# A causal attention and MLP-mixer kernel: loads of the opening in another sequence, and early work ordered to fit

## The chip, the cores and the metric

The kernel runs on one core of a Trainium2 chip. The metric is the device time of one execution in microseconds (us). The core has five engines that work side by side, each through its own queue in order: TensorE (PE, matrix products, with PEld for its weight loads), VectorE (DVE), ScalarE (ACT), GpSimd (POOL) and SyncE (SP), and DMA engines that move data between device memory and on-chip memory. PE writes its products into PSUM banks, which DVE and ACT empty.

## The reference

There are 8 batches of 576 positions with 8 heads of 64. Attention is causal by blocks of 64; its result goes through a token mixer and a channel mixer.

```
block_i, block_j = pos[:, None] // 64, pos[None, :] // 64
scores = q @ k^T / sqrt(64);  scores = where(block_i >= block_j, scores, -1e9)
attn   = exp(scores - max);   attn = attn / (sum(attn) + 1e-9)
x      = (attn @ v), heads side by side                 # 8 x 576 x 512
h      = relu(x^T @ w_tok1) @ w_tok2                     # 576 -> 256 -> 576
u      = x + h^T
out    = u + relu(u @ w_ch1) @ w_ch2                     # 512 -> 1536 -> 512
```

All inputs and the output are float32. Products are in bf16.

## The kernel before

The work is held as about 1590 numbered operations (`P.add`), each with its engine or a choice of engines, the operations it depends on, the PSUM banks it takes and gives back, and a function that issues its instructions. A table, `ORDER`, written out as a string, says in which order they are issued, on which engine (S, P, D, A, T for SP, POOL, DVE, ACT, PE), and in which banks: letters a to d are the four banks `mm`, e to h the four `late`, s and t two double banks in which the first scores are made. The late banks are the same memory as the double ones, and can be used only when the exps of the last double bank are done. `Plan.placed` walks through the table. Since each engine works in order, an operation that waits holds back all that stands behind it on its engine.

Batches go through the same steps, with the steps of neighbouring batches mixed. The loads of q, k (L418) and V (L468) stand on POOL's queue, which also converts them to bf16; so do the loads of the weights: w_tok1 and w_tok2 (L479), w_ch1 in eight pieces (L502) and w_ch2 in three (L511). Only the very first pieces of q and k go another way. The rest of the attention:

- q and k are transposed on DVE (`STREAM_TRANSPOSE`, L442). A score set (L568) holds the products of four heads (two at the start) for a part of the keys.
- exp is done on ACT (L587 for the double banks, L774 for the others) into `e_sb`. The part of `e_sb` that the mask leaves out is copied and cleared (L596, L601) on DVE or POOL.
- A head's output is the product of `e_sb` and V (L618, the odd ends in L671). DVE takes the reciprocal of the sum (L638, L693) and scales (L644, L699) into `x_sb`.

The mixer:

- `token_up`: x times w_tok1 (L809, L813), relu into `aT` on ACT (L795) or DVE (L797).
- batch 0 makes u^T on PE directly (L842, L857, emptied by L874 on DVE or its like on ACT). The others make u = x + h^T (L904, added on DVE in L919) and then transpose it (L991 for batch 1).
- channel up: u times w_ch1 (L1032 for batch 0), relu into `gT`.
- channel down: batch 0 uses a scheme of seven products for a 2 by 2 split (L1366), with sums of blocks of w_ch2 (`weight_sums`, L1318, four instructions on DVE into `wd_sb`, which need all three loads of w_ch2) and of `gT` (L1348); the later channel-up products use sums of blocks of w_ch1 (L1063) in the same way.

At the start PE runs products on zeros (`raise_clock`): one run of 11 products of 512 columns (L371), and single fillers of 256 columns (L378), 37 of which the table places between the first real products.

Of the kernel before, what the change touches and what calls it, by code (L numbers as in the profile page):

```python
# [27 lines left out]
class Plan:  # L28
# [73 lines left out]
    47Tb 48Tb 49Ta 50Ta 37P 51Ta 52Ta 53Ta 54Ta 55Ta 56Ta 35P 57Ta 7D 174Tst 175T 34P 195A 58Ta 59Ta 60Ta  # L102
    61Ta 196A 62Ta 38P 197D 63Ta 31D 64Ta 65Ta 66Ta 176A 199Tt 36P 177A 178D 67Ta 179D 68Ta 33D 69Ta 255P 70Ta 200A
    180Ts 27D 198P 71Ta 72Ta 40P 73Ta 181A 29D 182Tt 157P 74Ta 75Ta 76Ta 183A 77Ta 201Ts 43P 78Ta 79Ta 80Ta 253D
    202A 42P 214Tt 254D 188Tb 189T 41P 215A 184Tc 11D 233Ts 6D 190D 191D 258P 192Td 211Ta 234A 220Tt 216P 256D 39P
    185T 257D 221A 81Tb 218Ts 155P 212D 213D 207Tb 235D 208T 186D 219A 158P 187D 237Tt 193D 209D 156P 203Ta 210D
    204T 238A 194D 239Ts 261P 205D 206D 164P 8D 240A 236D 269Tcbda 424P 271A 163P 281Tefgh 270A 166P 259D 273A 217D
    226Tb 283A 227T 284A 222Tc 223T 228D 241Ta 242T 282A 229D 165P 249Tf 224D 245Tg 285A 225D 162P 246T 230Tb 243D
    244D 339Tc 159P 250D 231D 232D 337Ta 251D 247D 161P 340A 260D 272A 276Tbfeh 338D 348Tc 262D 160P 278A 349T 263D
    345Ta 280A 346T 248D 277A 341Td 350D 421P 301Tgbfh 274D 347D 264P 343Tc 342D 303A 275D 351Ta 304A 265P 352T 344D  # L110
    305A 425D 354Td 355T 302A 313Tcbfh 279A 356D 306P 387Tg 353A 267P 426D 384Td 315A 388T 266P 316A 404Ta 385T 317A
    268P 408Tb 314A 381Te 386D 405A 416Tf 427P 409D 390Tc 389A 307P 391T 333D 430P 372Td 392A 308Tabhg 167P 373T
    311A 334D 382T 168P 310A 369Tc 309A 370T 169P 417A 375Tb 335D 434P 312A 378Ta 379T 383A 433P 366Th 374A 367T
    422D 371A 436P 400Td 423D 376T 380A 289Tc 377A 295Ta 290D 298Tf 368A 291D 330Tb 296D 401A 297D 292Tc 299D 286Tg
    331D 332D 438Tadeh 300D 287D 293D 288D 324Tb 440A 294D 357Tf 325D 439A 321Tc 326D 363Tg 428D 442A 364T 322D 441A
# [67 lines left out]
def kernel(  # L183
# [95 lines left out]
    WARM, KEEP = 11, 110  # L279
    HALF_UP, FAST_UP = 1, 4  # L280

    def uT_of(b):
# [1284 lines left out]
```

## Time and profile before

Three runs took 283.47, 284.16 and 284.64 us (median 284.16).

| | before |
|---|---|
| profiled execution, its own time | 284.69 us |
| its span, from first to last instruction | 282.9 us |
| granted clock of PE (share of full speed) | 1.0 |
| batch 2's first score set starts on PE | 43.69 us |
| the first of the four sums of w_ch2 starts on DVE | 50.80 us |
| batch 0's channel down starts on PE | 55.75 us |
| bytes that the POOL queue moved | 17.49 MB |

In a row of the timeline the first number is the start in us, the second the time from the start of the first to the end of the last instruction that the row takes together; then the engine, the line of the kernel, the operation, its output and inputs with their shapes, and how many. A bracket at the end holds the idle time of the engine ahead of it, and what ended it. Rows of DMA issues give the size and the time from issue to landing. In the table of stretches each engine has its busy time and the number of its instructions.

### The profile page before, as it was taken

To read this page: it belongs to the slowest core of one execution; us is meant where nothing else is said; L and a number is where in the kernel's file an instruction comes from. 1 tells how busy PE (TensorE), PEld (TensorE's weight loads), DVE (VectorE), ACT (ScalarE), POOL (GpSimd) and SP (SyncE) were. 2 spreads that over 40 slices of the span, in tenths; PEclk is the share of its full clock that TensorE was granted. 3 is DMA by queue.
4 is the path that set the end of the run, shared out by engine and by line. 5 is a ranking of instruction groups with operands and counts; after the bars stand their busy time and mean duration, and the time that the engine had idled before them with its cause. 6 is when DMAs were issued, how large, how long until landed. Compare 5 with 4: busy or idle time off the path is not lost.

```text
span 282.9 us, 9352 instructions
## 1 busy us (share of the span) xinstructions
PE 275.3 (97%) x3982; PEld 204.0 (72%) x3982; DVE 238.9 (84%) x515; ACT 179.2 (63%) x331; POOL 72.7 (26%) x126
## 2 busy tenths in 40 slices
PE   7899999999999999999999999999999999999994
PEld 3466556588776788986877658756789876568884
DVE  3688669999889998999998979859896997579984
ACT  3798788953998856897879866274533744652200
POOL 8895870511631351063232221000000000000000
PEclk9999999999999999999999999999999999999999
DMA  7999999954979492999598594100044502200157
GB/s 163 160 178 192 202 190 206 152 92 86 142 87 139 87 150 56 250 109 170 66 118 139 56 188 60 70 10 19 0 84 95 196 0 76 75 1 2 74 151 224
DMA packets 64890, 31.95 MB, mean 113 GB/s; under 512 B 53200, under 2 KB 55888, under 8 KB 64848
## 3 DMA queue, kind: packets, MB, share of 16 engines
q0 software_dynamic: 44896, 17.49, 53.6%
q1 hardware_dynamic: 19520, 13.21, 18.2%
q8 instruction: 31, 0.51, 0.7%
q10 hardware_dynamic: 432, 0.66, 0.7%
q14 instruction: 11, 0.09, 0.1%
HBM read 35.85 MB, written 9.44 MB: 160 GB/s over the span
## 4 chain that ended last, share of the span: by engine, by line
PE 87%; DMA 4%; ACT 3%; POOL 3%; DVE 1%; issue 1%; POOLq 0%; DVEq 0%
PE late L1366 23%; PE mm L1105 8%; PE mm L1232 7%; PE mm L1366 7%; PE late L1232 6%; PE mm L568 6%; PE late L1105 6%; DMA qk_sb<-in_k_dram 4%; PE mm L618 4%; PE mm L809 3%; PE mm L904 2%; PE late L904 2%; PE late L618 2%; PE mm L1032 2%; ACT e_sb L774 2%; PE late L809 2%
## 5 line engine op out<-in xcount | busy, mean ns | idle before, releaser
L774 ACT ACTIVATE e_sb<-mm 128x512 bf16<-128x512 f32 x82 | 46.6, 606 | 13.1 <-PE late L568 9.4
L774 ACT ACTIVATE e_sb<-late 128x512 bf16<-128x512 f32 x86 | 48.5, 609 | 9.0 <-PE late L568 8.2
L442 DVE STREAM_TRANSPOSE qk_sb<-qk_sb 128x288 int32<-128x288 int32 (+1 forms) x65 | 41.8, 694 | 4.9 <-DMA qk_sb<-in_q_dram 1.8
L468 POOL DMA_DIRECT2D vals<-in_v_dram x45 | 36.9, 832 | 4.5 <-PE mm L618 2.4
L1366 PEld LDWEIGHTS <-gT 128*128 128x128 bf16 x336 | 32.0, 98 | 5.6 <-issue 0.4
L1366 PEld LDWEIGHTS <-sums 128*128 128x128 bf16 x324 | 31.3, 98 | 5.3 <-issue 0.4
L568 PEld LDWEIGHTS <-qk_sb 32*64 32x64 bf16 (+1 forms) x1152 | 19.0, 103 | 14.8 <-issue 11.1
L568 PE MATMUL mm<-qk_sb 32*64 32x64 bf16 (+7 forms) x504 | 26.9, 277 | 0.1
L618 PEld LDWEIGHTS <-e_sb 128*128 128x128 bf16 x640 | 23.1, 97 | 5.3 <-issue 2.2
L568 PE MATMUL late<-qk_sb 32*64 32x64 bf16 (+7 forms) x504 | 26.2, 283 | 0.6 <-issue 0.3
L1366 PE MATMUL late<-wd_sb,gT 128*128 128x256 bf16 x168 | 20.7, 273 | 0.0
L1366 PE MATMUL late<-wd_sb,sums 128*128 128x256 bf16 x168 | 20.6, 273 | 0.0
L1105 PEld LDWEIGHTS <-ws_sb 128*128 128x128 bf16 x192 | 18.2, 98 | 3.1 <-issue 0.9
L618 PE MATMUL mm<-vals,e_sb 128*128 128x65 bf16 x450 | 19.8, 193 | 0.5 <-DMA vals<-in_v_dram 0.3
L644 DVE TENSOR_TENSOR x_sb<-mm,rinv 128x256 bf16<-128x256 f32 x45 | 18.7, 422 | 1.3
L1412 DVE TENSOR_TENSOR o_sb<-late,u_sb 128x512 f32<-128x512 f32 x22 | 15.0, 684 | 3.6 <-PE late L1366 3.6
L1232 PEld LDWEIGHTS <-ws_sb 128*128 128x128 bf16 x120 | 11.7, 98 | 8.6 <-issue 0.2
L1105 PEld LDWEIGHTS <-wc_sb 128*128 128x128 bf16 x144 | 15.3, 114 | 1.5 <-issue 0.4
L1366 PE MATMUL late<-wc_sb,gT 128*128 128x256 bf16 x132 | 16.2, 273 | 0.0
L596 POOL COPY vals<-e_sb 128x256 bf16<-128x256 bf16 (+1 forms) x11 | 4.3, 393 | 39.7 <-ACT e_sb L774 39.6
L400 ACT COPY mm<-late 128x512 f32<-128x512 f32 (+1 forms) x16 | 9.1, 570 | 8.1 <-PE late L1232 5.4
L795 ACT ACTIVATE gT<-mm 128x512 bf16<-128x512 f32 x21 | 12.6, 616 | 1.9 <-PE mm L1105 0.9
(198 smaller groups left out, 630.7 us busy)
## 6 DMA issues: line engine op xcount, KB each, us to landing
out_dram<-o_sb SPq DMA_DIRECT2D x19, 256.0 KB, 3.0
qk_sb<-in_k_dram POOLq DMA_DIRECT2D x14, 288.0 KB, 6.0
qk_sb<-in_q_dram POOLq DMA_DIRECT2D x14, 288.0 KB, 5.9
vals<-in_v_dram POOLq DMA_DIRECT2D x28, 128.0 KB, 4.5
out_dram<-o_sb SPq DMA_DIRECT2D x7, 512.0 KB, 3.8
wc_sb<-in_moe_w_ch_dram POOLq DMA_DIRECT2D x8, 192.0 KB, 7.5
wc_sb<-in_moe_w_ch_dram POOLq DMA_DIRECT2D x3, 512.0 KB, 10.5
vals<-in_v_dram POOLq DMA_DIRECT2D x15, 64.0 KB, 5.3
```

The source lines that it names most:

```text
L442: nc.vector.transpose(dst[:, 0:S, :] .rearrange("p s e -> p (s e)") .bitcast(I32) .rearrange("p (a k) -> p k a", k=NB)[:, k0:k1], raw2.bit ...
L468: nc.gpsimd.dma_start(out=t[128 - p : 128, J, hs, 0:64], in_=src)
L568: nc.tensor.matmul(out=home(n)[rows, c : c + w], lhsT=bar[r, 0] if j is None else kT[i][r, keys, par], rhs=bar[r, 1] if j is None else qT[ ...
L618: nc.tensor.matmul(out=u[:, I, 0:65], lhsT=e[:, h, c : c + 128], rhs=vt[:, J, head, 0:65], start=(J == 0), stop=(J == I),)
L644: nc.vector.tensor_tensor(out=xt[:, 0:4, 64 * head : 64 * head + 64], in0=u[:, :, 0:64], in1=ri[:, 0:4].to_broadcast([128, 4, 64]), op=MULT,)
L774: nc.scalar.activation(dst, bank_of(x), EXP, scale=scale)
L795: nc.scalar.activation(dst, src, RELU)
L809: nc.tensor.matmul(out=ps, lhsT=w1_sb[:, c, tt : tt + 255 : 2], rhs=xt[:, c, cols], start=(c == 0), stop=False)
L1105: nc.tensor.matmul(out=bank_of(bank)[:, 256 * o_ : 256 * o_ + 256], lhsT=x(o_, m), rhs=y[:, :, m, :], start=opens, stop=m == 1, skip_group ...
L1232: nc.tensor.matmul(out=bank_of(bank)[:, 128 * c : 128 * (c + step)], lhsT=x(m), rhs=y[:, c : c + step, m, :], start=opens, stop=m == 1, sk ...
L1366: nc.tensor.matmul(out=bank_of(bank)[:, 256 * i : 256 * i + 256], lhsT=x[:, kk, 128 * i : 128 * i + 128], rhs=y[:, kk], start=first and i ...
L1412: nc.vector.tensor_tensor(out=dst, in0=src, in1=other, op=ADD)
```

## The change

The first 392 of the 1518 places of the table are written in another order; behind them the operations follow as before, with other bank letters. No operation is added or taken away, and the sequence on SP is the same. In addition the first 22 of the single fillers issue two products of 128 columns instead of one of 256. The code after the table is three lines shorter, and two behind the fillers: L1318 before is L1316 after, L618 is L616.

The diff, with the table cut to its first rows:

```
 ORDER = """
     13S 22P 24P 5P 9D 2D 3P 16S 44Ta 12P 19S 10P 4P 30P 14D 15D 17A 32P 1D 26P 18D 20A 28P 0A 45Tb 23D 25D 21D 252P 46Tb
...
@@ -276,7 +273,7 @@
     EARLY = ("mm", "full")
     BANK = ("mm", "late mm", "full", "late")
     SEED = ("full", "late", "mm", "late mm")
-    WARM, KEEP = 11, 110
+    WARM, KEEP, HALVED = 11, 110, 22
     HALF_UP, FAST_UP = 1, 4
 
     def uT_of(b):
@@ -374,11 +371,12 @@
         for n in range(KEEP):
             bank = {"covers": False}
 
-            def emit(o, bank=bank):
-                nc.tensor.matmul(
-                    out=bank_of(bank)[:, 0:256], lhsT=zeros[:, 0:128], rhs=zeros[:, 0:256],
-                    start=True, stop=True,
-                )
+            def emit(o, bank=bank, w=128 if n < HALVED else 256):
+                for c in range(0, 256, w):
+                    nc.tensor.matmul(
+                        out=bank_of(bank)[:, c : c + w], lhsT=zeros[:, 0:128], rhs=zeros[:, c : c + w],
+                        start=c == 0, stop=True, skip_group_check=c > 0,
+                    )
 
             P.add(
                 "PE", 0.11, emit, pads["zeros"], 1e6, take=[(BANK, bank)], give=[bank], at=5.0 + 0.12 * n, until=20.0,
```

On POOL's queue, the loads from batch 0's V on (`vals`), with the token weights (`w1_sb`, `w1o_sb`, `w2_sb`) and batch 1's second pair of k and q. Before:

```order
L479 DMA w2_sb_72<-in_moe_w_tok2_dram 128x1152
L468 DMA vals_62<-in_v_dram 64x4x64
L468 DMA vals_62<-in_v_dram 128x4x64 x2
L418 DMA qk_sb_61<-in_k_dram 128x1152
L596 COPY vals_62<-e_sb1 128x128
L468 DMA vals_62<-in_v_dram 128x4x64
L479 DMA w1_sb_70<-in_moe_w_tok1_dram 128x4x256
L479 DMA w1o_sb_71<-in_moe_w_tok1_dram 64x256
L479 DMA w1_sb_70<-in_moe_w_tok1_dram 64x256
L418 DMA qk_sb_61<-in_q_dram 128x1152
```

After:

```order
L466 DMA vals_62<-in_v_dram 64x4x64
L466 DMA vals_62<-in_v_dram 128x4x64 x3
L477 DMA w1_sb_70<-in_moe_w_tok1_dram 128x4x256
L477 DMA w1o_sb_71<-in_moe_w_tok1_dram 64x256
L477 DMA w1_sb_70<-in_moe_w_tok1_dram 64x256
L594 COPY vals_62<-e_sb1 128x128
L477 DMA w2_sb_72<-in_moe_w_tok2_dram 128x1152
L416 DMA qk_sb_61<-in_k_dram 128x1152
L416 DMA qk_sb_61<-in_q_dram 128x1152
```

The four V loads stand together ahead of all token weights, and w_tok2, which stood ahead of them, and the load of k stand behind.

Further down on POOL's queue, w_ch1 (`wc1_sb`), batch 1's V, batch 2's k and q, and w_ch2 (`wc2_sb`). Before:

```order
L502 DMA wc1_sb_73<-in_moe_w_ch1_dram 128x768
L418 DMA qk_sb_61<-in_q_dram 128x1152
L502 DMA wc1_sb_73<-in_moe_w_ch1_dram 128x768 x7
L418 DMA qk_sb_61<-in_k_dram 128x1152
L468 DMA vals_62<-in_v_dram 128x8x64 x2
L596 COPY vals_62<-e_sb1 128x256
L468 DMA vals_62<-in_v_dram 128x8x64 x2
L468 DMA vals_62<-in_v_dram 64x8x64
L418 DMA qk_sb_61<-in_k_dram 128x1152
L601 MEMSET e_sb1 64x4x64
L418 DMA qk_sb_61<-in_q_dram 128x1152
L511 DMA wc2_sb_74<-in_moe_w_ch2_dram 128x2048 x3
```

After:

```order
L599 MEMSET e_sb1 64x2x64
L500 DMA wc1_sb_73<-in_moe_w_ch1_dram 128x768 x8
L466 DMA vals_62<-in_v_dram 128x8x64 x4
L466 DMA vals_62<-in_v_dram 64x8x64
L416 DMA qk_sb_61<-in_q_dram 128x1152
L416 DMA qk_sb_61<-in_k_dram 128x1152 x2
L416 DMA qk_sb_61<-in_q_dram 128x1152
L509 DMA wc2_sb_74<-in_moe_w_ch2_dram 128x2048 x3
```

w_ch1 is unbroken, batch 1's V follows it, and all four loads of batch 2's q and k stand behind that. The three loads of w_ch2 come after the same loads as before. The clear (`MEMSET`) of row one of the second piece was on DVE, and the clear and the copy that stood among the V loads went to DVE.

On DVE, where batch 0's heads end and the next k is transposed. Before:

```order
L644 TENSOR_TENSOR x_sb<-mm,rinv 128x4x64
L344 MEMSET vals 64x8
L601 MEMSET e_sb 64x2x32
L442 STREAM_TRANSPOSE qk_sb<-qk_sb 128x9x32
L601 MEMSET e_sb 64x2x32
L638 RECIPROCAL rinv<-mm 128x4
L644 TENSOR_TENSOR x_sb<-mm,rinv 128x4x64
```

After:

```order
L599 MEMSET e_sb 64x2x32
L341 MEMSET vals 64x8
L697 TENSOR_TENSOR x_sb<-mm,rinv 128x64
L636 RECIPROCAL rinv<-mm 128x4 x2
L642 TENSOR_TENSOR x_sb<-mm,rinv 128x4x64
L795 TENSOR_SCALAR aT<-mm 128x2x128
L636 RECIPROCAL rinv<-mm 128x4
L691 RECIPROCAL rinv<-mm 128x1
L697 TENSOR_TENSOR x_sb<-mm,rinv 128x64
L642 TENSOR_TENSOR x_sb<-mm,rinv 128x4x64 x2
L636 RECIPROCAL rinv<-mm 128x4
L440 STREAM_TRANSPOSE qk_sb<-qk_sb 128x9x32
```

The clear of `e_sb` that stood behind the transpose stands ahead of it, and the relu of the first token product (`aT`) stands between the head outputs.

On DVE, at the sums of w_ch2 (`wd_sb`) and of batch 0's `gT`, with batch 1's u behind them. Before:

```order
L797 TENSOR_SCALAR gT<-late 128x512
L1348 TENSOR_TENSOR sums<-gT 128x1536
L1318 TENSOR_TENSOR wd_sb<-wc_sb 128x1536 x2
L1318 TENSOR_TENSOR wd_sb<-wc_sb,wd_sb 128x1536 x2
L919 TENSOR_TENSOR u_sb<-mm,x_sb 128x512
L919 TENSOR_TENSOR u_sb<-late,x_sb 128x512
```

After:

```order
L795 TENSOR_SCALAR gT<-late 128x512
L1346 TENSOR_TENSOR sums<-gT 128x1536
L1316 TENSOR_TENSOR wd_sb<-wc_sb 128x1536
L795 TENSOR_SCALAR aT<-late 128x512
L1316 TENSOR_TENSOR wd_sb<-wc_sb 128x1536
L1316 TENSOR_TENSOR wd_sb<-wc_sb,wd_sb 128x1536 x2
L917 TENSOR_TENSOR u_sb<-mm,x_sb 128x512
L917 TENSOR_TENSOR u_sb<-late,x_sb 128x512
```

The relu of batch 1's second token product (`aT`), which was on ACT, stands between the first two sums of w_ch2.

On PE the scores of batch 1 stood ahead of batch 0's last heads; now heads 5 and 4 of batch 0 and the first token product stand ahead of them, and batch 1's first score set goes into the late banks.

More of the change, by code (lines that the diff above doesn't have):

```diff
@@ L106 @@
[L106 to L110, printed above, removed]
@@ L278 @@
     SEED = ("full", "late", "mm", "late mm")
-    WARM, KEEP = 11, 110
+    WARM, KEEP, HALVED = 11, 110, 22
     HALF_UP, FAST_UP = 1, 4
```

157 lines of the change are left out of this document (80 added, 77 removed).

## The prediction

> **What bounds the kernel now.** I read the page first, then a table of engine busy time by stretches of the span, then the rows of single engines at the places where TensorE (PE) stood.
>
> ```profile
> span 282.9 us, 9352 instructions
> PE 275.3 (97%) x3982; PEld 204.0 (72%) x3982; DVE 238.9 (84%) x515; ACT 179.2 (63%) x331; POOL 72.7 (26%) x126
> DMA  7999999954979492999598594100044502200157
> ```
>
> ```profile
> 20.00:33.00 13.00, 11.90 (x276) 8.24 (x273) 9.98 (x30) 10.41 (x21) 8.07 (x14) 1.00 1.18 196
> 33.00:45.00 12.00, 12.00 (x217) 7.87 (x216) 7.94 (x20) 9.93 (x20) 7.30 (x12) 1.00 1.52 195
> 45.00:57.00 12.00, 11.92 (x173) 6.47 (x171) 11.57 (x22) 11.99 (x25) 4.25 (x9) 1.00 1.44 172
> 57.00:120.00 63.00, 63.00 (x1127) 50.56 (x1125) 58.56 (x134) 46.77 (x92) 18.06 (x30) 1.00 0.91 120
> 120.00:200.00 80.00, 80.00 (x1299) 58.07 (x1296) 71.19 (x165) 56.56 (x109) 17.34 (x28) 1.00 0.66 90
> ```
>
> The first two numbers of a stretch are its length and PE's busy time. From 57 to 200 us PE has no idle at all, and its clock column is 1.00 everywhere. So the end of the kernel is: the time at which PE enters that dense stretch, plus a fixed amount of PE work. The change does not alter the work behind the start, so it can only move the entry. What is left to win is small: 13.00 − 11.90 = 1.10 us of idle between 20 and 33 us, nothing from 33 to 45, and 0.08 between 45 and 57. The row of DMA shares (40 slices of 7.07 us) shows nines from the second to the eighth slice: the loads run back to back from 7 to 56 us. The order of loads therefore decides only who waits, not when all of them are in.
>
> These are PE's rows where the 1.10 us lie, with two dense rows behind them for comparison (start, duration, then what ran; in brackets the idle time before it and what ended it):
>
> ```profile
> 20.18 0.55 PE L568 MATMUL mm<-qk_sb 32*64 32x320 bf16 x4
> 21.37 0.63 PE L568 MATMUL late<-qk_sb 32*128 32x512 bf16 x8 [0.30 <-ACT e_sb L587]
> 22.28 0.45 PE L618 MATMUL mm<-vals,e_sb 128*128 128x65 bf16 x9 [0.28 <-DMA vals<-in_v_dram]
> 22.93 0.81 PE L618 MATMUL mm<-vals,e_sb 128*128 128x65 bf16 x21 [0.21 <-DVE e_sb L601]
> 25.87 0.38 PE L568 MATMUL mm<-qk_sb 32*64 32x448 bf16 x1
> 26.45 0.40 PE L842 MATMUL mm<-ident,x_sb 128*128 128x128 bf16 x4
> ```
>
> Three named waits, 0.30 + 0.28 + 0.21 = 0.79 us, belong to the end of batch 0's attention: a PSUM bank that an exp frees, the last load of V, and a small clear of the probability tile. A score set that runs dense takes 26.45 − 25.87 = 0.58 us; the one at 20.18 took 21.37 − 20.18 = 1.19, which is 0.61 too long, 0.30 of it counted as idle already. So the rows show 1.10 + 0.31 = 1.4 us that PE lost there.
>
> **The change, part by part.** *V and the token weights come earlier.* The last piece of batch 0's V stood behind w_tok2 and a k load, both of 288 KB. Its issue, that of the w_tok1 loads behind it, and two later 288 KB loads in a row, which give the queue's pace (POOL's rows, then the issue-to-landing rows of the same five loads):
>
> ```profile
> 16.75 0.75 POOL L468 DMA_DIRECT2D vals<-in_v_dram  x1
> 17.48 0.75 POOL L479 DMA_DIRECT2D w_sb<-in_moe_w_tok_dram  x1
> 18.78 0.54 POOL L479 DMA_DIRECT2D w_sb<-in_moe_w_tok_dram  x1
> 34.66 0.58 POOL L418 DMA_DIRECT2D qk_sb<-in_k_dram  x1
> 35.54 0.55 POOL L418 DMA_DIRECT2D qk_sb<-in_q_dram  x1
> ...
> vals<-in_v_dram POOLq DMA_DIRECT2D x1, 64.0 KB, 5.5
> w_sb<-in_moe_w_tok_dram POOLq DMA_DIRECT2D x1, 256.0 KB, 6.1
> w_sb<-in_moe_w_tok_dram POOLq DMA_DIRECT2D x1, 32.0 KB, 5.1
> qk_sb<-in_k_dram POOLq DMA_DIRECT2D x1, 288.0 KB, 6.7
> qk_sb<-in_q_dram POOLq DMA_DIRECT2D x1, 288.0 KB, 7.4
> ```
>
> The pair landed at 34.66 + 6.7 = 41.4 and 35.54 + 7.4 = 42.9, so 288 KB take about 1.6 us. V's last piece landed at 16.75 + 5.5 = 22.3, which is the wait at 22.28; without two such loads ahead of it it lands at about 19.1. The last w_tok1 piece goes from 18.78 + 5.1 = 23.9 to about 20.7. PE now takes the heads of batch 0 and the first token product at 20.2 to 21.5, where before it took batch 1's scores. The V wait (0.28) goes. The clear's wait (0.21) goes as well: its clear stood on DVE behind a transpose of the next k and now stands ahead of it. The new wait is for w_tok1 at 20.7, when the three head operations ahead of it are just done: 0 to 0.3 us.
>
> *Batch 1's scores come later.* They now go into the late banks. Those open when ACT has finished the last paired exp:
>
> ```profile
> 17.35 3.97 ACT L587 ACTIVATE e_sb<-sc 128x1024 bf16<-128x1024 f32 x4
> ```
>
> That is 17.35 + 3.97 = 21.32, so the scores start at about 21.4, PE reaches them at about 21.5, and ACT idles for some 0.5 us instead of having scores ready. ACT is not what PE waits for in the next 10 us, except at the bank handovers. Together I take 1.1 of the 1.4 us as won by 33 us. The bounds are 0, if the new waits eat it, and 1.4.
>
> *Batch 2's q and k go back.* The four loads now stand behind w_ch1 and batch 1's V, the last one landing where the last of them did, 42.9. The first pair thus lands by 42.9 − 2 × 1.6 = 39.7. It is needed by the scores at 43.69, which with 1.1 us of lead want to start at 42.6:
>
> ```profile
> 43.69 0.33 PE L568 MATMUL mm<-qk_sb 32*64 32x320 bf16 x2
> 42.32 0.42 DVE L644 TENSOR_TENSOR x_sb<-mm,rinv 128x256 bf16<-128x256 f32 x1
> 38.25 1.25 DVE L442 STREAM_TRANSPOSE qk_sb<-qk_sb 128x288 int32<-128x288 int32 x2
> ```
>
> Two transposes took 1.25 us, so the k pair is turned at about 41.0 if DVE is free; but a scaled output of a head (0.42) stands behind them on DVE and frees a bank for these scores, with other heads between. My walk along DVE's new order ends at 42.4 to 42.9. The lead here is 0.8 to 1.1.
>
> *Where the lead meets a load that does not move.* This decides the sum. The three w_ch2 loads have the same loads ahead of them as before, so the third lands when it did. Its issue and delay, then DVE's chain that it feeds, the relu on ACT that the change moves to DVE, and two of PE's consumers:
>
> ```profile
> 38.16 0.53 POOL L511 DMA_DIRECT2D wc_sb<-in_moe_w_ch_dram  x1 [0.36 <-DMA vals<-in_v_dram]
> wc_sb<-in_moe_w_ch_dram POOLq DMA_DIRECT2D x1, 512.0 KB, 12.2
> 49.92 0.96 DVE L1348 TENSOR_TENSOR sums<-gT 128x1536 bf16<-128x1536 bf16 x1
> 50.80 1.82 DVE L1318 TENSOR_TENSOR wd_sb<-wc_sb 128x1536 bf16<-128x1536 bf16 x2
> 52.53 1.95 DVE L1318 TENSOR_TENSOR wd_sb<-wc_sb,wd_sb 128x1536 bf16<-128x1536 bf16 x2
> 54.66 0.69 DVE L919 TENSOR_TENSOR u_sb<-mm,x_sb 128x512 bf16<-128x512 f32 x1 [0.18 <-PE mm L904]
> 58.34 0.68 DVE L919 TENSOR_TENSOR u_sb<-mm,x_sb 128x512 bf16<-128x512 f32 x1
> 52.00 0.64 ACT L795 ACTIVATE aT<-mm 128x512 bf16<-128x512 f32 x1
> 55.75 0.49 PE L1366 MATMUL late<-wc_sb,gT 128*128 128x256 bf16 x3
> 59.36 0.39 PE L991 MATMUL mm<-ident,u_sb 128*128 128x128 bf16 x4
> ```
>
> The load landed at 38.16 + 12.2 = 50.4. The first weight sum (L1318) started at 50.80, when DVE came free: the load was hidden by 0.4 us. With a lead of about 1 us DVE comes free at 49.8 and waits for the load. The sum starts at about 50.4, and only 0.4 us of the lead is left on DVE. Behind that sum now stands the relu of batch 1's second token product, about 0.6 us on DVE for one of 512 columns by the pitch of its neighbours; before, ACT did it at 52.00. It ends at about 50.4 + 0.87 + 0.7 = 52.0, against 52.00 + 0.64 = 52.64 before: what needs it (a PSUM bank of a score set, a token product) may start 0.6 earlier, so this is not yet the limit. The other sums follow, then the three u rows. The 0.18 us for which DVE waited at 54.66 vanishes, and the fourth u row, which ended at 58.34 + 0.68 = 59.02, ends at 59.02 − 0.40 + 0.60 − 0.18 = 59.04, with a clear of 0.1 that also moved to DVE at 59.1. PE used it at 59.36. So PE can be at most about 0.25 us ahead there. Behind it PE is dense, and DVE in turn waits for PE: this lead stays to the end. I take 0.25 us. The bounds are −0.2, if the load lands 0.4 later, and 1.1, if DVE's chain does not hold PE.
>
> *The fillers.* Twenty-two PE fillers of 256 columns become pairs of 128. Nine of them stand ahead of a score set:
>
> ```profile
> 8.96 1.16 PE L378 MATMUL mm<-wd_sb 128*128 128x256 bf16 x9
> 10.20 0.39 PE L568 MATMUL sc<-qk_sb 32*64 32x448 bf16 x2
> 24.64 0.40 PE L809 MATMUL mm<-x_sb,w_sb 128*128 128x128 bf16 x4
> 24.88 0.19 PE L813 MATMUL mm<-x_sb,w_sb 128*128 128x64 bf16 x1
> ```
>
> Four products of 128 columns with their own weights take 24.88 − 24.64 = 0.24 us, 0.06 each, so eighteen take 1.08 us. The nine old ones took 10.20 − 8.96 = 1.24 us at most. Cost: 0. [...]
>
> **Sum.** The profiled execution took 284.69 us, 1.8 more than its span; it lies 0.53 above the median of 284.16. Its 284.69 − 0.25 = 284.44, by the median 283.9.
>
> **Rivals.** *The lead passes.* If the third w_ch2 load lands by 49.7, or PE has more slack to DVE's chain than I read, the 1.1 us stays: 283.1, and 282.8 at the bound of 1.4. For it: the loads that now stand together are larger, and the stretch with the weights (20 to 33) moved 196 GB/s against 172 from 45 to 57. Against: the bytes ahead are the same.
>
> *Slower: batch 2's first scores wait.* Their q and k landed long before use; now k lands at about 39.7 with two transposes and DVE's head outputs behind it. The point is a landing of 40.8 us: from there the scores start after 43.69, and each further us costs PE one, since the channel products that could cover have already run. At 42.0 it costs 1.2: 285.4. For it: DVE works in order, and everything behind the transpose stands too. Against: the last of the four loads landed at 42.9 already, and two of them stand behind this one.
>
> *The change wins nothing early.* If w_tok1 lands at 21.8 instead of 20.7, the first token product holds PE and, since its relu stands ahead of head outputs on DVE's queue, those too. The lead is then gone by 33 us, and the relu on DVE costs 0.2: 284.4.
>
> **How the numbers follow.** Forecast 0.46 (283.9, own range 283.5 to 284.3), the lead passes 0.25 (282.6 to 283.4), slower 0.16 (284.9 to 286), nothing early 0.13 (284.2 to 284.8). A measurement of this kernel can hardly tell less than 0.5% (1.42 us) from no change, so faster means under 282.74 and slower over 285.58. Faster: most of the lead's bound is needed, 0.16 of the 0.25 and a little for what I have not seen, 0.19. Slower: 0.10 of the 0.16 and 0.04 for what I have not seen, 0.14. The rest, 0.67, is within. The range 282.6 to 285.1 leaves out about 1 in 10 on either side.
>
> **What the profile after would show.** Right: PE's rows at 20 to 23 us without the waits for V and the clear; the V of batch 0 landing at 19 and w_tok1 by 21; batch 2's scores at 42.6 to 43.0; a wait of DVE's first weight sum (now L1316) for w_ch2, ended at about 50.4; the relu (L795) right behind it; the down product (now L1364) at 55.3 to 55.5, and no idle of PE from 57 on. Wrong: w_ch2's third load in by 49.7, or the weight sum without a wait before it (the lead passes); a wait of DVE's transposes (L440) for k near 40 to 42 us with PE idle before batch 2's scores (slower); PE idle before L807 or L811 at 21 us for w_tok1 (nothing early); the filler pairs at over 0.07 us each.

## The result, and the profile after

The changed kernel is slower. Its median is 288.77 us (five runs, 288.31 to 289.28), that of the kernel before on the same chip 284.16 (283.47 to 284.88): a ratio of 1.0144 (95% interval 1.0101 to 1.0187), 4.1 us more. The forecast was 283.9, 0.25 less. The profiled execution took 288.77 us; its span is 287.0 against 282.9.

The page of the kernel after, its span and busy times:

```profile
span 287.0 us, 9353 instructions
PE 276.3 (96%) x3982; PEld 205.7 (72%) x4004; DVE 239.4 (83%) x516; ACT 179.6 (63%) x331; POOL 72.2 (25%) x125
```

The work is the same; PE is busy 1.0 us longer by the page and idle for the rest. The stretches of the span, with the columns that the prediction explained:

```profile
20.00:33.00 13.00, 11.09 (x270) 8.07 (x268) 7.97 (x24) 9.80 (x20) 7.33 (x12) 1.00 1.11 187
33.00:45.00 12.00, 11.51 (x176) 7.12 (x170) 8.05 (x18) 10.16 (x21) 7.40 (x12) 1.00 1.53 194
45.00:57.00 12.00, 11.88 (x220) 6.69 (x217) 11.69 (x28) 10.92 (x23) 3.68 (x7) 1.00 1.50 194
57.00:120.00 63.00, 62.04 (x1089) 49.75 (x1095) 58.31 (x131) 45.98 (x90) 18.53 (x31) 1.00 0.87 107
120.00:200.00 80.00, 79.01 (x1301) 57.93 (x1307) 70.77 (x164) 56.24 (x108) 17.51 (x28) 1.00 0.72 99
```

Two things stand here that the forecast did not have. The stretch from 20 to 33 us has more idle time than before (1.91 us against 1.10). And from 57 to 200 us, where PE had none, it now has 0.96 + 0.99 us. (PE's 22 missing instructions make the idle time of this trace look a little larger; another profile of the same kernel, with all 4004, the third in the table below, shows 0.61 + 0.54.)

Idle time alone is a rough measure, because short pauses inside a group of products count as busy. A sharper one is the **lag**: the start of one and the same PE operation in this trace, less its start in the first trace of before. It was worked out from the timelines, at six operations that before ran at these times. In the opening the two kernels issue PE's operations in different orders; the operation at 31.26 us (the second product of the last pair of L857, L855 after) is one ahead of which both have issued the same ones. The second profile of after is that of e9 below, the third that of e14.

```
before, us                    31.26  57.15  59.88  129.88  182.11  275.20
after                         +0.19  +1.13  +1.58   +2.45   +3.65   +3.84
after, second profile         +0.05  +0.12  +0.55   +1.16   +2.34   +2.52
after, third profile          +0.04  +0.10  +0.55   +1.68   +2.87   +3.07
```

So the loss has three parts: what the opening leaves at 57 us, which scatters from 0.1 to 1.1; a step of 0.43 to 0.45 at 59.88 us; and 2.0 to 2.5 us in the dense stretch behind it, where the table's operations stand in the same order as before. This third part is the largest, and the prediction had it at nothing.

How it looks from near. One operation of the channel-up product at 185 us in the kernel after, on PE and then on DVE, and the same two pieces in the kernel before:

```profile
184.87 0.59 PE L1230 MATMUL late<-uT,wc_sb 128*128 128x512 bf16 x2
185.76 0.59 PE L1230 MATMUL mm<-uT,wc_sb 128*128 128x512 bf16 x2 [0.30 <-DVE x_sb L642]
...
185.29 0.42 DVE L642 TENSOR_TENSOR x_sb<-mm,rinv 128x256 bf16<-128x256 f32 x1
```

```profile
181.68 1.03 PE L1232 MATMUL mm<-uT,wc_sb 128*128 128x512 bf16 x4
181.93 0.76 DVE L644 TENSOR_TENSOR x_sb<-mm,rinv 128x256 bf16<-128x256 f32 x2
```

Before, four products run without a pause, while DVE scales two head outputs beside them. After, the second two wait until DVE has scaled a head output (185.29 + 0.42 = 185.71). They have no use for that output: they want the PSUM bank that it stood in. DVE does the same work at the same point; the table now hands PE this bank at this place, where before it handed out one that had been emptied earlier. In the table the place reads `1279Tba` (operation 1279, on PE, banks b and a) where it read `1279Ted`.

PE's waits of 0.2 us or more in the kernel after, from 60 to 200 us (before has none there), and then the larger of its waits up to 60 us that are new:

```profile
PE mm L1230 <- DVE x_sb L642: 0.3, 1, 0.3
PE late L989 <- DVE u_sb L917: 0.2, 1, 0.2
PE late L902 <- DVE x_sb L642: 0.2, 1, 0.2
```

```profile
PE late L840 <- DVE x_sb L697: 0.7, 1, 0.7
PE mm L807 <- DMA w_sb<-in_moe_w_tok_dram: 0.7, 1, 0.7
PE late L1030 <- DMA wc_sb<-in_moe_w_ch_dram: 0.5, 1, 0.5
PE late L566 <- DVE aT L795: 0.3, 1, 0.3
```

The first list is far shorter than 2 us. The rest comes in about a dozen steps of 0.04 to 0.28 us, most of which no list of waits shows; the lag finds them, because it compares the same operation in two traces. The larger ones, with the instruction that ended last before the operation could start, in the first and third profile of after, and in two experiments that are told below:

```
           before
operation  at, us   after  third   e2     e10    released by
852        121.1    0.09   0.08   0.08    -      a head output on DVE
862        123.5    0.16   0.15   0.16    -      a head output on DVE
1011       163.7    0.29   0.28   0.28   0.28    a head output on DVE
1197       175.6    0.10   0.10   0.10   0.10    a head output on DVE
1279       182.1    0.47   0.46   0.26   0.27    a head output on DVE
```

The same operations lose the same, to about 0.01 us, in each of these profiles, but for 1279, which loses less in e2 and e10: that is no chance, but the sequence.

### The profile page after: what moved, and what is told of

It reads as the page before. It is cut to its first block, busy times and chain, and to the rows that moved or that the text cites. A ratio compares the mean times of both kernels' runs of the same rounds, so it can differ in the third digit from the quotient of the medians.

```text
span 287.0 us, 9353 instructions
## 1 busy us (share of the span) xinstructions
PE 276.3 (96%) x3982; PEld 205.7 (72%) x4004; DVE 239.4 (83%) x516; ACT 179.6 (63%) x331; POOL 72.2 (25%) x125
## 3 DMA queue, kind: packets, MB, share of 16 engines
q1 hardware_dynamic: 19520, 13.21, 19.1%
## 4 chain that ended last, share of the span: by engine, by line
PE 71%; DVE 8%; issue 1%; ACT 1%; DVEq 0%
PE late L1364 16%; PE mm L1364 11%; PE late L1103 7%; PE late L1230 7%; PE mm L1230 6%; PE mm L1103 6%; PE late L566 3%; PE mm L566 3%; PE mm L616 2%; PE late L616 2%; PE late L807 2%; PE mm L807 2%; PE late L902 1%; DVE u_sb L917 1%; DVE wd_sb L1316 1%
## 5 line engine op out<-in xcount | busy, mean ns | idle before, releaser
L772 ACT ACTIVATE e_sb<-mm 128x512 bf16<-128x512 f32 x96 | 53.4, 607 | 11.9 <-PE mm L566 7.2
L772 ACT ACTIVATE e_sb<-late 128x512 bf16<-128x512 f32 x72 | 41.5, 610 | 11.0 <-issue 4.1
L616 PEld LDWEIGHTS <-e_sb 128*128 128x128 bf16 x640 | 23.7, 97 | 5.6 <-issue 3.0
L566 PE MATMUL mm<-qk_sb 32*64 32x64 bf16 (+7 forms) x560 | 26.8, 282 | 0.3
L566 PE MATMUL late<-qk_sb 32*64 32x320 bf16 (+7 forms) x448 | 25.3, 277 | 0.3 <-DVE aT L795 0.3
L616 PE MATMUL mm<-vals,e_sb 128*128 128x65 bf16 x370 | 17.0, 193 | 0.3
L1103 PEld LDWEIGHTS <-wc_sb 128*128 128x128 bf16 x144 | 15.3, 114 | 1.4 <-issue 0.4
L1364 PE MATMUL late<-wd_sb,sums 128*128 128x256 bf16 x132 | 16.2, 273 | 0.0
L642 DVE TENSOR_TENSOR x_sb<-mm,rinv 128x256 bf16<-128x256 f32 x37 | 15.4, 420 | 0.9
L793 ACT ACTIVATE gT<-late 128x512 bf16<-128x512 f32 x21 | 12.3, 612 | 3.2 <-PE late L1103 2.6
L1410 DVE TENSOR_TENSOR o_sb<-late,u_sb 128x512 f32<-128x512 f32 x17 | 11.4, 682 | 3.0 <-PE late L1364 3.0
L1230 PEld LDWEIGHTS <-wc_sb 128*128 128x128 bf16 x90 | 10.0, 113 | 5.5 <-issue 0.6
L416 POOL DMA_DIRECT2D qk_sb<-in_k_dram x14 | 7.7, 552 | 22.9 <-DVE qk_sb L440 13.7
```

The source lines that it names most:

```text
L566: nc.tensor.matmul(out=home(n)[rows, c : c + w], lhsT=bar[r, 0] if j is None else kT[i][r, keys, par], rhs=bar[r, 1] if j is None else qT[ ...
L616: nc.tensor.matmul(out=u[:, I, 0:65], lhsT=e[:, h, c : c + 128], rhs=vt[:, J, head, 0:65], start=(J == 0), stop=(J == I),)
L642: nc.vector.tensor_tensor(out=xt[:, 0:4, 64 * head : 64 * head + 64], in0=u[:, :, 0:64], in1=ri[:, 0:4].to_broadcast([128, 4, 64]), op=MULT,)
L772: nc.scalar.activation(dst, bank_of(x), EXP, scale=scale)
L793: nc.scalar.activation(dst, src, RELU)
L1103: nc.tensor.matmul(out=bank_of(bank)[:, 256 * o_ : 256 * o_ + 256], lhsT=x(o_, m), rhs=y[:, :, m, :], start=opens, stop=m == 1, skip_group ...
```

## The experiments

Before's times were taken on the same chip each time. All in one table, the lag by each run's own profile (a dash: not read there):

```
                    median    ratio  95%             lag at  31.26  57.15  59.88  129.88  182.11  275.20
e1  banks before    286.22   1.0048  1.0014-1.0081          -0.22  -0.03  +0.41   +0.92   +0.94   +0.94
e2  banks after     285.74   1.0044  1.0008-1.0079          -1.09  -1.09  -1.03   -0.42   +0.58   +0.58
e3  loads alone     298.30   1.0457  1.0410-1.0505          +5.75  +14.1  +14.1   +14.1   +14.1   +14.1
e4  w_tok2 back     288.03   1.0105  1.0057-1.0153          -0.01  +0.06  +0.51   +1.40   +2.59   +2.78
e11 the same again  288.59   1.0164  1.0128-1.0199          +1.42  +1.49  +1.93   +3.10   +4.29   +4.50
e9  after again     288.09   1.0145  1.0112-1.0177          +0.05  +0.12  +0.55   +1.16   +2.34   +2.52
e10 banks half      286.89   1.0086  1.0060-1.0112          -0.75  -0.57  -0.13   -0.13   +0.88   +0.87
e5  fillers         284.56   0.9986  0.9953-1.0019          -1.06  -0.95  -0.95   -0.94   -0.94   -0.93
e6  e1, relu back   286.35   1.0060  1.0032-1.0088          -0.24  +0.15  +0.44   +0.44   +0.44   +0.43
e7  e6, w_tok2 back 286.75   1.0070  1.0046-1.0095            -      -      -       -       -       -
e13 tok later       285.87   1.0028  0.9997-1.0060          -0.70  +0.57  +0.86   +1.21   +1.20   +1.20
e8  before, V,clear 284.19   0.9978  0.9952-1.0004          -0.03  -0.03  -0.03   -0.03   -0.03   -0.03
e12 the same again  284.50   0.9993  0.9968-1.0018          +0.20  +0.20  +0.20   +0.20   +0.20   +0.20
```

**The banks (e1, e2).** The sequence differs in the first 393 places, but behind them 211 of the 226 places that name banks name other ones. To tell the opening from the banks, e1 takes after's opening with before's banks behind it, and e2 the reverse. Since the banks that are free differ where the two are joined, the letters of the second part are renamed as a whole; the sequence in which they come round is that of its own kernel.

```diff
 e1 (against after), two of its places:
-862Tf ... 1279Tba
+862Tg ... 1279Tde
 e2 (against before):
-862Tg ... 1279Ted
+862Tf ... 1279Tbh
```

> The changed kernel up to place 393 of the table, and from there on the same operations with the bank letters of the kernel before (renamed so that the banks still held at that place agree). Theory (banks): between 70 and 262 us the changed kernel loses 2.2 us in about fifteen small steps, each where PE waits for a PSUM bank that DVE or ACT has just emptied, because the later part of the table hands out the banks in another sequence. Then PE is dense again from about 62 us on and the time is about 286.5 us. Rival (late): DVE and ACT are late from the opening and PE pays for that in steps, whatever banks it has: 288.8 us, the steps stay.

> The kernel before up to place 393, and from there on the bank letters of the changed kernel, renamed in the same way. Theory (banks): the opening is as before, and PE loses about 2 us between 70 and 262 us: 286.2 us. Rival (late): banks cost nothing when the opening is in time: 284.2 us, PE idle under 0.1 us from 57 to 200 us.

With before's banks the slowdown falls from 1.44% to 0.48%: by the ratios, (1.0144 − 1.0048) × 284.2 = 2.7 us. By the lag, after loses 2.26 us between 59.88 and 275.20 (1.97 and 2.52 in its other profiles), and e1 0.53, which is one step: a pause of 0.52 us in the middle of a head's products at 93.5 us, for which the trace names no wait. That pause is not the banks' (the last section has it). Without it, the three profiles of after lose 2.0 each (0.25 and 0.53 of the first and third are this pause), and e1 nothing. With after's banks behind before's opening, e2 loses 1.61 us (−1.03 to +0.58) where before loses nothing. The stretches of e1 and then of e2:

```profile
57.00:120.00 63.00, 62.41 (x1112) 49.80 (x1111) 58.26 (x132) 45.98 (x91) 17.69 (x30) 1.00 0.89 111
120.00:200.00 80.00, 80.00 (x1303) 58.37 (x1302) 71.75 (x166) 56.59 (x110) 17.51 (x28) 1.00 0.69 97
```

```profile
57.00:120.00 63.00, 62.98 (x1125) 50.55 (x1122) 58.30 (x135) 46.83 (x91) 17.75 (x29) 1.00 0.90 120
120.00:200.00 80.00, 79.66 (x1276) 57.81 (x1261) 70.66 (x161) 55.48 (x108) 17.11 (x27) 1.00 0.74 87
```

From 120 to 200 us e1 is without idle time, as before was. In e2 PE meets the pause at operation 1279 again, in another physical bank than in after (`1279Tbh` against `1279Tba`): its four products, dense in 1.03 us before, take 1.28.

```profile
182.00 1.28 PE L1229 MATMUL late<-uT,wc_sb 128*128 128x512 bf16 x4
```

So it is not a bank as such that is slow, but how recently the one handed out was emptied.

**Half of the banks (e10).** After, with before's banks for the places 393 to 839 only (58 to 132 us), its own, renamed, behind.

```diff
-862Tf ... 1279Tba
+862Tg ... 1279Tfd
```

> The changed kernel with the bank letters of the kernel before from place 393 to place 839 of the table (about 58 to 132 us), and its own letters, renamed to fit, behind that. Theory (banks, each step local): the steps between 62 and 132 us go, 0.9 us in the first trace, and those behind 132 us stay, 1.4 us: the time lies between e1 and the changed kernel, about 1.1 us under the latter. Rival (the steps follow from DVE being late once): all of them go, as in e1, or all stay.

The lag is −0.13 from 59.88 to 129.88, then grows to +0.88 by 182 us. In after, it grows by 0.6 to 1.1 us up to 129.88, which are gone here, and by 1.4 behind it, of which 1.0 is left. The loss goes where the banks go, and that settles the largest part.

**The same kernels again (e9, e14, e15).** e9 and e14 are the kernel after, e15 is the kernel before; e14 and e15 have a single run each.

> The changed kernel itself, beside the others of this call. If its opening is as slow as in its first trace whenever it runs, the third w_ch2 load lands at 52.5 to 53 us again and the time is 288.8 us. If part of that was chance (e1 and e6 have the same loads in the same order and landed it at 51.7), it lands near 51.7 us, PE is at most 0.5 us behind the kernel before at 57 us, the steps by the banks stay, and the time is 287.2 to 288 us.

> The changed kernel, one more look, to see how far its opening scatters: PE's lag at 57 us was 1.1 and 0.1 us in its two traces. The steps by the banks behind 60 us should again come to 1.9 to 2.2 us.

> The kernel before, one more look, for the same reason: with its opening in e2 and e5, PE was 1 us earlier at 57 us than in its first trace. If that is common, the opening before is on the average ahead of the changed one by half a microsecond; behind 60 us PE should lose nothing.

The ratio comes again (1.0145). What the opening leaves does not: the lag at 57.15 us was 1.13, 0.12 and 0.10 in three profiles of one kernel. In the profiles of e15 (287.56 us) and of e7 below PE's granted clock was 0.50 from about 16 to 26.5 us, and no lag is read from them.

**The loads alone (e3).** Before's work in before's order on all other engines; on POOL the loads in after's order, up to the third load of w_ch2 (43, 42, 41 and 39 are V of batch 0, 157 is w_tok2, 258 and 261 are k and q of batch 1, 424 and 421 a k and a q of batch 2).

```diff
-40P 157P 43P 42P 41P 258P 216P 39P 155P 158P 156P 261P 164P 424P 163P ...
+40P 43P 42P 41P 39P 155P 216P 158P 156P 157P 258P 261P 164P 163P ... 268P 424P 421P
```

> The kernel before with the changed sequence of loads on POOL's queue alone, up to the third load of w_ch2; the work of the other engines and the banks as before. Theory (queue pace): the last four V pieces in a row, which POOL takes 0.75 us each to issue and which are 128-byte packets, leave the queue half empty from 17 to 19 us, and the large loads behind them no longer share the engines with small packets; the third w_ch2 load lands at 52.5 to 53 us instead of 50.3, DVE's sums of w_ch2 start 2 us later and the time is 285.7 to 286.7 us. Rival (same bytes, same pace): it lands at 50.3 us, and the time is 283.9 to 284.6 us; the late landing in the changed kernel then came from POOL's other work.

It costs 13 us, far outside both ranges. The third w_ch2 load landed at 54.6 us, but that is not where the time goes. Stretches of 1 to 6 us:

```profile
31.00:32.00 1.00, 1.00 (x14) 0.91 (x12) 0.12 (x1) 0.87 (x2) 0.92 (x2) 0.50 1.14 200
32.00:33.00 1.00, 1.00 (x39) 0.74 (x38) 0.90 (x3) 0.07 (x1) 0.31 (x1) 0.80 1.17 202
...
37.60:44.00 6.40, 0.91 (x10) 0.26 (x3) 1.26 (x3) 2.96 (x7) 6.28 (x12) 0.89 0.85 121
44.00:46.00 2.00, 1.97 (x7) 0.88 (x7) 0.58 (x1) 0.00 (x0) 0.86 (x2) 0.50 1.10 204
46.00:48.00 2.00, 2.00 (x11) 1.14 (x10) 0.79 (x2) 1.08 (x2) 0.55 (x1) 0.50 1.12 221
48.00:50.00 2.00, 2.00 (x11) 1.01 (x9) 1.97 (x3) 0.00 (x0) 0.00 (x0) 0.63 1.09 219
```

and the two waits with what DVE did meanwhile:

```profile
26.99 1.33 PE L615 MATMUL mm<-vals,e_sb 128*128 128x65 bf16 x21 [4.80 <-DVE e_sb L598]
44.03 1.01 PE L1029 MATMUL mm<-uT,wc_sb 128*128 128x512 bf16 x2 [5.52 <-DVE uT L871]
...
26.04 0.72 DVE L439 STREAM_TRANSPOSE qk_sb<-qk_sb 128x288 int32<-128x288 int32 x1 [5.65 <-DMA qk_sb<-in_k_dram]
42.74 0.72 DVE L439 STREAM_TRANSPOSE qk_sb<-qk_sb 128x288 int32<-128x288 int32 x1 [6.19 <-DMA qk_sb<-in_q_dram]
```

A transpose of k that now lands late stands ahead of a clear that PE needs; DVE works in order, so a head waits 4.80 us for a load that has nothing to do with it. The same happens once more with q and `uT` (5.52). Then, behind each wait, the clock column is 0.50 for some 5 us. The reordered work of the change is thus not an extra: it is what keeps the new loads from costing 13 us.

**w_tok2 back ahead of V (e4, e11).** After, with only that one load moved back. e11 is the same kernel beside e9.

```diff
-40P 43P 42P 41P 39P 155P 158P 156P 216P 157P 258P
+40P 157P 43P 42P 41P 39P 155P 158P 216P 156P 258P
```

> The changed kernel with one load moved: w_tok2 stands in front of the last four V pieces again, as in the kernel before. Theory (queue pace): large packets run beside the small ones again; V is in at 19.5 to 20 us, w_tok1 at 21 to 21.5 us as in the changed kernel although 288 KB more are ahead of it, and the third w_ch2 load lands 1 to 1.6 us earlier, at 51.3 to 51.9; the time is 287.3 to 288.1 us. Rival (same bytes, same pace): w_tok1 lands 1.6 us later, at 23, PE waits that much longer at 21 us, and w_ch2 lands as in the changed kernel at 52.9: 289 to 290 us.

> The kernel of e4 (w_tok2 in front of the last V pieces, the changed kernel else), beside the changed kernel on the same chip. Theory (queue pace): w_ch2 lands 0.7 us or more earlier than in e9, and the time is 0.5 to 1.2 us under e9. Rival: no difference beyond 0.3 us, e4's advantage was chance.

In the first run it seemed better than after (1.0105); beside e9 on one chip it is not (1.0164 against 1.0145). The third w_ch2 load landed earlier than in the profiles of after (51.0 and 50.8 against 52.9, 51.3 and 51.7), and the time did not improve. (In e11's profile PE's granted clock was 0.50 from 23.4 to 26.8 us, so its lag is not that of the loads alone.)

**The relu back on ACT (e6, e7).** e1, with the relu of batch 1's second token product (operation 505) issued on ACT again, ahead of the other relu; e7 with w_tok2 back as well.

```diff
-170D 503A 471A 505D 472A 445Tfegb 514Th 171D
+170D 505A 503A 471A 472A 445Tfegb 514Th 171D
```

> The changed opening with the bank letters of the kernel before (as in e1), and the relu of batch 1's second token product back on ACT, ahead of the first one's relu. Theory (DVE chain, step of the prediction): without the 0.6 us between the sums of w_ch2, PE's wait for the last u row at about 60 us (0.41 us in e1) goes, and the time is 0.3 to 0.5 us under e1: 285.8 us. Rival (the third w_ch2 load alone sets the chain, at 51.7 us or later): the wait stays at 0.3 us or more, time as e1, 286.2 us.

> The changed opening with three parts undone: bank letters, the relu on DVE, and w_tok2 in front of the last V pieces. If the three costs add up (2.6 + 0.4 + 1.0 us of about 4.2) the time is 284.7 us, the kernel before within 0.3. Rival (they overlap, since each is a wait of PE that hides another): 285.5 us or more. What is left over would be the rest of the opening: scores and heads in another order, q and k of batch 2 late.

No gain in time (1.0060 and 1.0070 against 1.0048, the intervals overlap). By the lag, the step at 59.88 us is 0.29 in place of 0.44.

**The first token product later (e13).** e6, with the rest of head 5 of batch 0 (227), batch 1's first score set (269) and the odd ends of batch 0's heads (249) ahead of the first token product (337), whose relu stands later on DVE, behind two more instructions of the heads.

```diff
-223T 337Tc 269Tefgh 227T 249Ta
+223T 227T 269Tefgh 249Ta 337Tc
```

> e6 (changed opening, bank letters before, relu on ACT) with the first token product moved: PE takes the second half of head 5 and batch 1's first scores ahead of it, and its relu stands two head outputs later on DVE. Theory (the wait for w_tok1 at 21 us, 0.8 to 1.1 us on PE, and DVE standing behind it, are what the opening costs): PE is 0.5 us or more ahead of e6 at 33 us and still 0.3 us or more ahead behind 60 us: 285.6 us or less. Rival (the prediction's step: what is won early is given back at the third w_ch2 load): PE is ahead at 33 and 44 us, and within 0.15 us of e6 behind 60 us: 286.2 us.

The wait for w_tok1 goes, and waits of 0.5 us for a relu and for V come. PE is 0.46 us ahead of e6 at 31.26 us, but 0.42 behind it at 57.15, so neither forecast holds for the traces. The median ratio, 1.0028, is the smallest of all kernels with the new loads, and its interval reaches to no change; it does not separate from e1.

**The fillers (e5), and V and the clear (e8, e12).** Before, with the halved fillers alone; and before, with the last piece of batch 0's V (39) ahead of the k load (258) and the clear (217) ahead of the transpose (259) on DVE, which is the part of the change that takes two named waits away.

```diff
 e5:
-    WARM, KEEP = 11, 110
+    WARM, KEEP, HALVED = 11, 110, 22
 e8, e12:
-258P ... 39P      259D 273A 217D
+39P ... 258P      217D 273A 259D
```

> The kernel before with the first 22 fillers halved and nothing else. By the changed kernel's trace a filler pair takes 0.11 us like the single one, so nothing changes: 284.0 to 285.0 us beside the kernel before at about 284.5. Rival (pairs cost 0.05 us more each, or they let the clock fall): the score set behind the nine fillers starts 0.2 us later or the clock column shows less than 1.0, and the time is 0.2 to 1 us longer.

> The kernel before with two small moves: the last piece of V ahead of the k load of batch 1's second half, and on DVE the clear of the probability tile ahead of that k's transpose. Theory (waits at 22 us are real and what follows is dense): the waits of 0.28 and 0.21 us go, PE is 0.4 to 0.6 us earlier at 24 us and stays so: 0.4 us under the kernel before. Rival (a lead is given back at the third w_ch2 load, as my forecast had it): under 0.2 us of it is left behind 60 us.

> The kernel of e8 once more, to see whether it beats the kernel before: 0.3 to 0.9 us under it if e8's 0.6 us was more than chance, within 0.2 us of it if not.

Neither moves the time. In e8 and e12 both waits at 22 us are gone. (A wait for another piece of V comes earlier there, which before's first trace does not have:

```profile
15.45 0.40 PE L615 MATMUL mm<-vals,e_sb 128*128 128x65 bf16 x8 [0.70 <-DMA vals<-in_v_dram]
```

this is e8's.) From the score set at 21.37 us to the token product at 24.64 before took 3.27 us, and e8 and e12 take 3.12 each: of the 0.49 us of the two waits, 0.15 are won. In e2 and e5, whose opening has before's loads and order, the two waits are missing too, and the stretch takes the same 3.12. No version beat the kernel before.

## Why the prediction was wrong

**The step that failed: "plus a fixed amount of PE work. The change does not alter the work behind the start, so it can only move the entry."** The order of the work behind the start is the same, but not its banks, and the description of the change says so. PE was without a pause in this stretch only because each bank it was handed had been emptied in time; the slack in this is small, so another sequence of banks gives other waits. This costs 2.0 us by the traces of after, 1.6 in e2, and 2.7 by the medians (after against e1, which holds some chance). An estimate before the run was within reach: the places of the table show which operation gave back each bank last, and before's trace when that operation ended. Nobody tried whether it would have come out near 2 us.

**"The lead here is 0.8 to 1.1."** There was none: at 31.26 us after lags by 0.19, 0.05 and 0.04 in its three profiles. (The first loses another 0.9 us by 57 us, 0.49 of it in the wait for w_ch1.) The rows of PE and DVE in after:

```profile
21.07 0.40 PE L807 MATMUL mm<-x_sb,w_sb 128*128 128x128 bf16 x4 [0.67 <-DMA w_sb<-in_moe_w_tok_dram]
27.48 0.38 PE L840 MATMUL late<-ident,x_sb 128*128 128x128 bf16 x4 [0.69 <-DVE x_sb L697]
...
22.02 0.42 DVE L795 TENSOR_SCALAR aT<-mm 128x256 bf16<-128x256 f32 x1 [0.88 <-PE mm L811]
22.95 0.18 DVE L636 RECIPROCAL rinv<-mm 128x4 f32<-128x4 f32 x1 [0.51 <-PE mm L616]
25.93 0.72 DVE L440 STREAM_TRANSPOSE qk_sb<-qk_sb 128x288 int32<-128x288 int32 x1 [1.52 <-DMA qk_sb<-in_k_dram]
27.23 0.19 DVE L697 TENSOR_TENSOR x_sb<-late,rinv 128x64 bf16<-128x64 f32 x1
```

The V wait and the clear's wait at 22 us went, as forecast. "The new wait is for w_tok1 [...]: 0 to 0.3 us" was 0.67 (0.6 and 0.9 in the other two profiles): the pieces landed at 21.0 to 21.4 and not at 20.7, and PE was ready at 20.40, so both ends of that term were off. So the first half of the rival "the change wins nothing early" came in (chance 0.13, priced at 284.4): PE waits for w_tok1, and DVE stands 0.88 us for the relu. Its second half did not: no head output was ready behind the relu, since DVE then stands another 0.51 us for PE's next head. What PE waits for at 27.48 has another cause, for which the prediction has no term. The `x_sb` that it needs (L697) stands on DVE behind the transpose of batch 1's k, and DVE stood 1.52 us for that load. Before, the load stood ahead of w_tok1 and landed at 21.9; now it stands behind w_tok2 and landed at 25.9. In the other two profiles it landed at 25.5 and 25.2, DVE waited 1.05 us and not at all, and PE 0.21 us and not at all. What remained of it at 57 us cannot be given well: in five profiles with after's opening untouched (after, e9, e14, e1, e10) the lag there is on average +0.15, in five with before's (before itself, e2, e5, e8, e12) −0.37, and both kinds scatter over more than 1 us. Half a microsecond is likely, and not settled. Removing the two waits at 22 us by themselves (e8, e12) won 0.15 of their 0.49 us, and e2 and e5 do not have them at all. So "1.1 of the 1.4 us as won" was too much from the start: the waits were read from a single profile, and a wait of PE counts only if what follows is not waiting as well.

**"The order of loads therefore decides only who waits, not when all of them are in."** The size was wrong. The issues on POOL's queue in after, and its DMA engines from 15 to 29 us in after and then in before:

```profile
13.19 2.84 POOL L466 DMA_DIRECT2D vals<-in_v_dram  x4 [0.73 <-DMA qk_sb<-in_k_dram]
39.71 0.53 POOL L509 DMA_DIRECT2D wc_sb<-in_moe_w_ch_dram  x1 [0.36 <-DMA vals<-in_v_dram]
...
wc_sb<-in_moe_w_ch_dram POOLq DMA_DIRECT2D x1, 512.0 KB, 13.2
```

```profile
DMA packets 3897, 2.28 MB, mean 163 GB/s; under 512 B 2395, under 2 KB 3482, under 8 KB 3895
```

```profile
DMA packets 4145, 2.60 MB, mean 185 GB/s; under 512 B 2513, under 2 KB 3598, under 8 KB 4142
```

Four pieces of V of 64 KB in a row take 0.71 us each to issue, and in that stretch the queue moves 163 GB/s against 185 (167 and 166 in e9 and e14; 193 and 180 in e2 and e5, which have before's loads). The third w_ch2 load landed at 39.71 + 13.2 = 52.9 and not at 50.4 (51.3 and 51.7 in e9 and e14). w_ch1 was complete at 36.0 and not at 34.8, and PE waited 0.5 us for it, at L1030; in e9 and e14 it was in by 34.5 and 34.9, without that wait.

**"Where the lead meets a load that does not move. This decides the sum."** Wrong in two ways. The load did move, and it decided nothing. DVE's first two weight sums in after, in e2 (third load in at 50.3) and in e13 (52.4):

```profile
52.09 0.95 DVE L1316 TENSOR_TENSOR wd_sb<-wc_sb 128x1536 bf16<-128x1536 bf16 x1
52.96 0.68 DVE L795 TENSOR_SCALAR aT<-late 128x512 bf16<-128x512 f32 x1
53.56 0.95 DVE L1316 TENSOR_TENSOR wd_sb<-wc_sb 128x1536 bf16<-128x1536 bf16 x1
```

```profile
49.71 1.82 DVE L1315 TENSOR_TENSOR wd_sb<-wc_sb 128x1536 bf16<-128x1536 bf16 x2
```

```profile
51.31 0.95 DVE L1317 TENSOR_TENSOR wd_sb<-wc_sb 128x1536 bf16<-128x1536 bf16 x1
52.46 0.96 DVE L1317 TENSOR_TENSOR wd_sb<-wc_sb 128x1536 bf16<-128x1536 bf16 x1 [0.20 <-DMA wc_sb<-in_moe_w_ch_dram]
```

After starts the first sum at 52.09, 0.8 us before the third load is in; e2 starts it 0.6 us ahead of the landing. The first sum reads only the first half of w_ch2, which the first two loads bring; it is the second that needs the third load, as its wait in e13 shows, the only one of its kind in the traces. (The description of the kernel before says that all four sums need all three loads; that is so in the table's dependencies, not in what the instructions wait for.) Before, the second sum started at 50.80 + 1.82 − 0.95 = 51.67, so the cover was 51.67 − 50.4 = 1.3 us, not 0.4, and a lead of 1 us passes: e2 and e5 had leads of 1.09 and 0.95 at 57 us and kept 1.03 and 0.95 at 59.88.

**The u row behind the relu** was the right place with the right chain, but as a cost and not as a cap. Every profile with after's DVE order there shows a step of 0.43 to 0.45 us at 59.88 us, whether PE led by 0.57 (e10) or lagged by 1.13 (after), because all that stands ahead on DVE moves with PE. In e1, where PE is at −0.03, the fourth u row starts at 59.02 against 58.34: 0.46 of that stands there already at the first three rows (the relu, less a wait that it fills), 0.21 is the clear. PE had 0.3 us of slack. With the relu on ACT (e6) the step is still 0.29: the second u row then waits 0.24 us for an exp on ACT.

**What was right.** V's last piece landed at 18.9 (forecast about 19.1; 19.3 and 20.0 in e9 and e14). The fillers cost nothing. PE's rows in after:

```profile
8.49 1.18 PE L376 MATMUL mm<-wd_sb 128*128 128x128 bf16 x18
9.73 0.39 PE L566 MATMUL sc<-qk_sb 32*64 32x448 bf16 x2
```

From the first filler to the next score are 9.73 − 8.49 = 1.24 us, as with the nine whole ones, so a product of 128 columns takes at most 1.24 / 18 = 0.07 us there, and e5 measured no difference (0.9986, 95% interval 0.9953 to 1.0019). The slower rival did not occur: PE has no wait ahead of batch 2's first scores.

**The sum.** In after's first trace: opening 1.13, the u row's chain 0.45, banks 2.0, the pause at 93.5 us 0.25, and 0.27 behind 275 us, together the 4.1 of the span. In its other two profiles the opening is 0.1, so that this part is chance to a large degree. By the medians 2.7 of 4.1 us are the banks; the 1.4 left in e1 (0.4 to 2.3) are the chain's 0.4 and about 1 us, of which the traces place half in the opening and some in the pause, and the rest stays open. e1's 1.4 and e2's 1.25 us (0.2 to 2.2) do not add up to 4.1; the intervals allow that they do, and whether opening and banks together cost more than each alone was not tried.

## What to carry to other kernels

In a stretch where PE has no idle time, the order in which buffers are handed out is part of the schedule: a change that leaves the order of work alone and deals out the banks anew is not neutral (here it cost 2.0 us by the traces), and each place should be asked who emptied that bank last, and when. Compare two traces by the start of the same operation, not by idle time: many small steps (here of 0.04 to 0.28 us) show in no list of waits. And before an early gain is counted, check that it is still there at the entry to the part that is bound, and that it is larger than the scatter between two profiles of one kernel (here 1 us).

## What the runs showed of the hardware that was not expected

**The clock after an idle stretch.** In e3, PE stood for 4.80 and 5.52 us, until 26.99 and 44.03. Its granted clock was 0.50 from 25.6 to 32.4 us and from 42.6 to 49.5 us, so it fell while PE stood, and PE worked 5.4 us at 0.50 each time. Two products of 512 columns take 1.01 us there (44.03 us), against 0.59 at a clock of 1.00 (51.50 us in the same trace). By an estimate that takes 0.50 for half speed, each wait was up to 2.7 us dearer than its length, 15.7 us in all; the lag grows by 14.1.

A wait need not be that long, though. These are a stretch of e11 and one of e15, with PE's busy time and, third from the end, the clock:

```profile
23.40:26.80 3.40, 3.40 (x75) 3.04 (x59) 2.16 (x9) 2.06 (x4) 1.94 (x5) 0.50 1.12 194
16.50:26.70 10.20, 10.08 (x174) 5.97 (x165) 5.17 (x20) 7.35 (x10) 7.97 (x16) 0.50 1.31 173
```

In the 3.4 us ahead of each (as long as e11's stretch) PE had waited 1.16 and 0.48 us (e11) and 0.24 and 0.75 us (e15), and was busy for about half and 70% of that time. In e15 the clock then stayed at 0.50 for 10.2 us, though PE hardly paused. In other traces waits of this size had no such sequel (0.97 and 0.30 us within 1.6 us in e12). What decides it stays open.

**A pause without a named wait.** In e1 and in after's third profile, inside one head output:

```profile
93.53 0.33 PE L616 MATMUL late<-vals,e_sb 128*128 128x65 bf16 x5 [0.35 <-issue]
```

```profile
93.88 0.65 PE L616 MATMUL mm<-vals,e_sb 128*128 128x65 bf16 x16 [0.37 <-issue]
```

PE stops half-way through ten products of one head and waits for nothing that the trace shows. It is at the same head, with 0.25 to 0.57 us, in after, e14, e4, e11, e1 and e13, and missing in e9, which is the same kernel as after, and in e2, e5, e6, e8, e10 and e12. All that have it have the new opening; none with before's order of work does (before, e2, e3, e5, e8, e12). Its cause is open.

**The opening scatters.** Three profiles of one kernel differ by 1.0 us at 57 us, and five of before's opening by 1.3, while behind 60 us, banks being equal, they run alike to 0.05 us but for that pause. Most of it is loads that land at other times (batch 1's k at 25.9, 25.5 and 25.2 us in the three profiles of after, the third of w_ch2 at 52.9, 51.3 and 51.7); which comes late differs from run to run. Before's first trace also has a pause of 0.32 us at 28.8 us, without a named wait, that e2, e5 and e12 do not have.
